# Decode attention on one core: 4 MB slabs of four kv heads in four slots, a softmax per two slabs, and the diagonal of PV picked on the vector engine

## The chip, the cores and the metric

The kernel runs on one core of a Trainium2 chip. The metric is the device time of one execution in microseconds. Most executions of a kernel agree within 0.3%; medians are quoted, and the state of each run (fast, slow, or unknown for a single run) is respected where kernels are compared. Ratios are the mean time of one kernel's fast runs over that of the other's fast runs in the same rounds on the same chip, so they are not quite the ratios of the medians quoted beside them.

## The reference

Two independent problems (A and B) of the same shape. Each is one decode step of attention with a sliding window:

```
B, Sq, D = 2, 1, 576;  Hq, Hkv, Sk, Dh = 32, 16, 16384, 128;  W = 4096
q = (x @ wq) as [B, Hq, 1, Dh]
k = repeat(k_cache[:, :, Sk-W:, :], 2)        # v likewise
scores = q k^T * Dh**-0.5;  p = softmax(scores);  o = p v
result = o as [B, 1, Hq*Dh] @ wo              # A and B joined on the last axis
```

Everything is bf16. The windows of K and V are 134 MB, the four weight matrices 19 MB. Each byte is used once, so the kernel is a stream of loads with some arithmetic beside it.

## The kernel before

All work is recorded as operations on five queues (PE tensor, DVE vector, ACT scalar, POOL, SP for the loads). The order of the `S.add` calls of one engine is the order in which that engine runs them; waits are derived from the dependency lists. A slab is one kv head of both batches: 128 rows of 16 KB, 2 MB. Slabs of K and V go through a ring of eight slots. A K slab is transposed in two halves on the vector engine (X), multiplied with the queries on PE (S); after four slabs comes one softmax (maximum, exponential, transpose of the probabilities pT); a V slab is multiplied seven slabs later (PV).

```python
    NR = 8; NXT = 3; LAG = 7           # ring slots, buffers for transposed halves, slabs between S and PV
        def make_X(t, jb):             # transpose of half a K slab: vector engine
            n = 2 * t + jb
            deps = [stream_dma[("K", t)]]
            if n >= NXT:
                pn = n - NXT
                deps.append(Sop[(pn // 2, pn % 2)])       # buffer free: three halves back
            ...
            Xop[(t, jb)] = S.add("dve", lambda e: e.transpose(xt[:, n % NXT, :].bitcast(FP32), ring[...]), deps, ...)
            if jb == 1:
                last_reader[("K", t)] = Xop[(t, jb)]      # the slot may be loaded again
        def make_S(t, jb): ...         # 8 matmuls of 512 columns, needs Xop[(t, jb)]
        def make_evac(G, pr):          # PV sums out of PSUM: scalar engine
            evac_op[(G, pr)] = S.add("act", lambda e: e.activation(oE[:, pr, :], OTB[:, :], ACTF.Copy, scale=rsb[...]), deps, ...)
        def make_dg(G):                # diagonal picked by 8 fp32 matmuls
            ...
        for t in range(NSLAB + LAG + 1):                  # NSLAB = 32
            i = t - LAG
            make_X(t, 0); make_S(t, 0)
            if Gc is not None: make_chain(Gc)             # every fourth step
            if Gp is not None: make_dg(Gp)                # every fourth step
            make_X(t, 1); make_S(t, 1)
            ...                                           # make_chain2, make_PV(i), make_chain3, make_evac, make_proj
```

(Conditions on `t` are left out in the loop.)

## Time and profile before

| | before |
|---|---|
| time, median | 367.23 us (367.14 to 367.76, three runs; 367.31 us over the four runs taken beside the kernel after) |
| span of the profiled run | 365.9 us |
| loaded | 153.1 MB |
| mid-kernel rate, 60 to 330 us | 427 GB/s, DMA share 1.01 |
| DVE busy | 51% |

These lines are from the page of the profiled run. In the slices each digit is the busy share of one fortieth of the span, in tenths; the line of queue q1 gives packets, MB and the share of the 16 DMA engines' span; a group's line gives busy us, mean ns of one, and then the engine's idle time just before these instructions and what ended it.

```profile
span 365.9 us, 3683 instructions
...
PE 273.0 (75%) x1700; PEld 101.6 (28%) x1435; DVE 185.8 (51%) x189; ACT 34.3 (9%) x114; POOL 14.2 (4%) x53
...
DMA  8999999999999999999999999999999999999995
...
q1 hardware_dynamic: 11236, 153.10, 98.7%
...
DMA 81%; DVE 12%; PE 5%; ACT 1%; issue 1%; SPq 0%
...
L436 DVE STREAM_TRANSPOSE xt<-ring 128x2048 f32<-128x2048 f32 x64 | 144.3, 2286 | 84.5 <-DMA ring<-in_A_k_cache_dram 43.3
```

The DMA engines work from the second slice to the last but one. The vector engine's transposes (L436) sit idle 84.5 us, and what ends it is a landing of K: the engine waits for data, and data come as fast as they can. The windows view (busy us per engine, PE clock, DMA share, GB/s) of mid-kernel says it in one line:

```profile
60.00:330.00 270.00, 211.75 (x1072) 75.27 (x856) 149.51 (x143) 23.41 (x79) 7.04 (x24) 0.82 1.01 427
```

### The profile page before, as it was taken

Reading aid. Unit: us, or ns where it says so; the run is one execution under the profiler, and the core shown is the slowest. Engines: PE = TensorE matmul, PEld = TensorE weight load, DVE = VectorE, ACT = ScalarE, POOL = GpSimd, SP = SyncE. Lnnn points to the kernel's source line nnn. Section 1 sums busy time; section 2 is a strip of 40 time slices with the busy share of each in tenths; the row PEclk is TensorE's granted clock in tenths of the full one; section 3 lists DMA queues with packets and bytes.
Section 4 is the critical chain, followed back from the end, with each engine's and each line's share of the span. In section 5 each row is a group of like instructions: output and inputs, shape, how many; then the busy total and the mean of one; then the engine's idle time right before and its main releaser. Section 6 shows DMA issues by size and latency. Waiting matters only on the chain.

```text
span 365.9 us, 3683 instructions
## 1 busy us (share of the span) xinstructions
PE 273.0 (75%) x1700; PEld 101.6 (28%) x1435; DVE 185.8 (51%) x189; ACT 34.3 (9%) x114; POOL 14.2 (4%) x53
## 2 busy tenths in 40 slices
PE   0635874967859888597867688596797977597796
PEld 0311111112215322252213232152224322143544
DVE  2105988955743675436644477405764467234100
ACT  1011002002000020002000020000300020002100
POOL 5010000000000000000000000000000000000000
PEclk9998999896995889858998869859897689959959
DMA  8999999999999999999999999999999999999995
GB/s 323 451 410 428 430 428 422 436 424 424 430 424 430 428 430 428 421 430 429 428 424 433 428 426 424 428 426 428 430 424 425 428 430 430 424 427 426 427 414 205
DMA packets 11264, 153.34 MB, mean 419 GB/s; under 512 B 1256, under 2 KB 1392, under 8 KB 2032
## 3 DMA queue, kind: packets, MB, share of 16 engines
q1 hardware_dynamic: 11236, 153.10, 98.7%
q8 instruction: 12, 0.20, 0.2%
q14 instruction: 4, 0.03, 0.0%
q10 hardware_dynamic: 12, 0.01, 0.0%
HBM read 153.10 MB, written 0.00 MB: 418 GB/s over the span
## 4 chain that ended last, share of the span: by engine, by line
DMA 81%; DVE 12%; PE 5%; ACT 1%; issue 1%; SPq 0%
DMA ring<-in_B_k_cache_dram 41%; DMA ring<-in_A_k_cache_dram 28%; DVE xt L436 11%; DMA wob<-in_B_wo_dram 8%; DMA ring<-in_A_wq_dram 4%; PE st L460 1%; PE st L380 1%; PE ot L273 1%; PE tb L619 1%; ACT pR L511 1%; PE pj L682 0%; DVE pT L530 0%; SPq L372 0%; PE tb L500 0%; DVE out_sb L692 0%
## 5 line engine op out<-in xcount | busy, mean ns | idle before, releaser
L436 DVE STREAM_TRANSPOSE xt<-ring 128x2048 f32<-128x2048 f32 x64 | 144.3, 2286 | 84.5 <-DMA ring<-in_A_k_cache_dram 43.3
L460 PE MATMUL st<-xt,zq 128*128 128x512 bf16 x256 | 114.7, 448 | 60.1 <-DVE xt L436 60.0
L380 PE MATMUL st<-xt,zq 128*128 128x512 bf16 x256 | 114.9, 449 | 0.0
L460 PEld LDWEIGHTS st<-xt,zq 128*128 128x128 bf16 x256 | 28.4, 111 | 154.7 <-DVE xt L436 82.8
L584 PE MATMUL ot<-ring,pT 128*32 128x512 bf16 x448 | 57.2, 407 | 0.7 <-ACT oE L609 0.7
L584 PEld LDWEIGHTS ot<-ring,pT 128*32 128x32 bf16 x448 | 21.0, 102 | 35.5 <-issue 18.4
L619 PEld LDWEIGHTS tb<-selv,oE 128*128 128x128 f32 x112 | 22.1, 293 | 6.0 <-issue 4.2
L619 PE MATMUL tb<-selv,oE 128*128 128x16 f32 x112 | 21.0, 335 | 0.8 <-ACT oE L609 0.8
L423 POOL TENSOR_TENSOR zq<-qs,bmask 128x64 bf16<-128x64 bf16 x32 | 9.3, 294 | 272.3 <-PE st L380 173.9
L638 DVE TENSOR_TENSOR oA<-tb,cmask 128x256 bf16<-128x256 f32 x7 | 3.0, 425 | 30.7 <-PE tb L619 30.7
L609 ACT ACTIVATE oE<-ot,rsb 128x512 f32<-128x512 f32 x14 | 9.6, 685 | 76.9 <-PE ot L584 76.9
L511 ACT ACTIVATE pR<-st,bias_sb 128x256 bf16<-128x256 f32 x32 | 15.9, 544 | 0.3
L470 DVE TENSOR_REDUCE mx<-st 128x2 f32<-128x512 f32 x16 | 10.0, 664 | 2.6 <-PE tb L650 2.6
L682 PE MATMUL pj<-wob,oP 128*2 128x288 bf16 x126 | 10.1, 305 | 0.9 <-DMA wob<-in_B_wo_dram 0.6
L530 DVE STREAM_TRANSPOSE pT<-pR 128x512 bf16<-128x512 bf16 x16 | 10.4, 686 | 0.0
L654 ACT ACTIVATE oP<-tb 128x16 bf16<-128x16 f32 x8 | 1.5, 191 | 92.7 <-PE tb L650 92.7
L254 PE MATMUL tb<-ident_b,xt 2*128 2x2 bf16 x36 | 2.3, 194 | 9.9 <-DVE xt L221 9.9
L504 ACT ACTIVATE bias_sb<-tb 128x2 f32<-128x2 f32 x8 | 1.4, 172 | 89.2 <-PE tb L500 89.2
L500 PE MATMUL tb<-ones_f,nMrep 1*128 1x1 f32 x32 | 5.2, 263 | 6.1 <-DVE nMrep L494 6.1
L593 PEld LDWEIGHTS st<-pT,ring 128*128 128x128 bf16 x256 | 7.2, 100 | 6.2 <-DMA ring<-in_B_v_cache_dram 6.1
L593 PE MATMUL st<-pT,ring 128*128 128x16 bf16 x256 | 7.6, 172 | 1.4 <-DMA ring<-in_B_v_cache_dram 1.3
L485 DVE TENSOR_REDUCE nM<-tb 1x8 f32<-1x64 f32 x16 | 2.7, 207 | 11.4 <-PE tb L476 11.4
(67 smaller groups left out, 89.6 us busy)
## 6 DMA issues: line engine op xcount, KB each, us to landing
ring<-in_A_k_cache_dram SPq DMA_DIRECT2D x16, 2048.0 KB, 33.1
ring<-in_A_v_cache_dram SPq DMA_DIRECT2D x16, 2048.0 KB, 35.1
ring<-in_B_k_cache_dram SPq DMA_DIRECT2D x16, 2048.0 KB, 35.8
ring<-in_B_v_cache_dram SPq DMA_DIRECT2D x15, 2048.0 KB, 35.2
ring<-in_A_wq_dram SPq DMA_DIRECT2D x1, 4608.0 KB, 13.4
ring<-in_B_wq_dram SPq DMA_DIRECT2D x1, 4608.0 KB, 23.8
wob<-in_A_wo_dram SPq DMA_DIRECT2D x4, 1152.0 KB, 32.4
wob<-in_B_wo_dram SPq DMA_DIRECT2D x3, 1152.0 KB, 30.4
```

The source lines that it names most:

```text
L380: return e.add_instruction(mybir.InstMatmult(name=nc.get_next_instruction_name(), engine=mybir.EngineType.PE, ins=[e.lower_ap(mv), e.lower ...
L423: return e.tensor_tensor(dst, src, msk, ALU.mult)
L436: Xop[(t, jb)] = S.add("dve", lambda e: e.transpose(xt[:, n % NXT, :].bitcast(FP32), ring[:, r, jb * HW_:(jb + 1) * HW_].bitcast(FP32)), d ...
L460: last = e.matmul(st[bk][:, 0:512], wt, mv, start=first, stop=True, skip_group_check=True)
L470: mxs = [S.add("dve", lambda e, jb=jb: e.tensor_reduce(mx[:, jb, :], st[jb][:, :].rearrange("p (x t) -> p t x", t=2), AX.X, ALU.max), [Sop ...
L511: last = e.activation(pR[:, jb, :].rearrange("p (x t) -> p t x", t=2)[:, t, :], st[jb][:, :].rearrange("p (x t) -> p t x", t=2)[:, t, :], ...
L530: chain[(G, "pT%d" % jb)] = S.add("dve", lambda e, jb=jb: e.transpose(pT[:, v, 512 * jb:512 * jb + 512].rearrange("p (w j q) -> p j w q", ...
L584: last = e.matmul(OTB[32 * c:32 * c + 32, :], pT[:, v, col:col + 32], ring[:, r, j * 128:(j + 4) * 128], start=(j % 32 == 0), stop=(j % 32 ...
L593: last = e.matmul(OL[m % 2][:, 0:16], ring[:, r, j * 128:(j + 1) * 128], pT[:, v, col:col + 16], start=(j == 0), stop=(j == KR - 1))
L609: evac_op[(G, pr)] = S.add("act", lambda e: e.activation(oE[:, pr, :], OTB[:, :], ACTF.Copy, scale=rsb[:, v, pr:pr + 1]), deps, "oE%d_%d" ...
L619: last = e.matmul(bank[:, 0:16], oE[:, pr, 128 * c:128 * c + 128], selv[:, pr, c, :], start=(pr == 0 and c == 0), stop=(pr == 1 and c == 3))
L682: last = e.matmul(PJ[half], oP[:, v, j, :], wob[:, v, j, half * NH:(half + 1) * NH], start=(proj_start(G) and j == 0), stop=True, skip_gro ...
```

## The change

The intent: fewer and larger loads (32 slabs of 4 MB with 32 KB rows), fewer small instructions. A slab is now four kv heads of one batch. There are four slots of 4 MB instead of eight of 2 MB, two buffers for transposed halves (of twice the size) instead of three, and one softmax per two slabs. The PV sums are no longer copied by the scalar engine and put through 112 fp32 matmuls: the vector engine multiplies them by a mask of the diagonal while it empties PSUM, and adds up. The core of the diff (start-up, masks, weights and the emission of waits are cut):

```diff
-    NR = 8
-    NXT = 3
-    LAG = 7
+    NSLOT = 4
+    LAG = 3
...
-            src = src_t[:, g, Sk - W:Sk, :].rearrange("b (r j) d -> r b (j d)", j=KR)        # 16 KB rows
+            src = src_t[b, 4 * g:4 * g + 4, Sk - W:Sk, :].rearrange("k (r j) d -> r k j d", j=KJ)  # 32 KB rows
...
+        def make_X(t, jh):
+            deps = [stream_dma[("K", t)][0][2], Sop[(t - 1, jh)] if t >= 1 else op_xT]
+            Xop[(t, jh)] = dve(lambda e: e.transpose(
+                xt[:, jh, :].bitcast(FP32).rearrange("p (kp x kt) -> p x kp kt", kp=2, kt=2),
+                ring[:, r, jh * HW_:(jh + 1) * HW_].bitcast(FP32).rearrange("p (x kp kt) -> p x kp kt", kp=2, kt=2)), ...)
...
+        def make_bias(G):
+            n, bk, op = tb_job(lambda e, bank: e.transpose(bank[:, 0:1], nMrep..., ident_f[0:1, 0:1]), ...)   # PE
+            b4 = dve(lambda e: e.scalar_tensor_tensor(bias4[:], vmask[:], bk[:, 0:1], offm[:], ALU.mult, ALU.add), [op, ...], ...)
...
+        def make_evac(i):
+            evac_op[i] = dve(lambda e: e.scalar_tensor_tensor(tv, o, rsb[:, v, b:b + 1], dm, ALU.mult, ALU.mult), deps, "ev%d" % i)
+            ch[(G, "red%d" % b)] = dve(lambda e: e.tensor_reduce(oR[:, b, :], tmp..., AX.X, ALU.add), ...)
...
+        def make_dg(G):
+            n, bank, op = tb_job(lambda e, bank: e.matmul(bank[:, 0:256], selx..., oR..., start=True, stop=True), ...)   # PE
+            a = dve(lambda e: e.tensor_tensor(tmp[:, 0:256]..., bank[:, 0:256]..., cm16..., ALU.mult), [op, d_cm, ch["tmp"]], ...)
+            ch[(G, "oP")] = dve(f_pick, [a] + ..., "oP%d" % G)
...
+        for t in range(NSLAB + LAG):          # NSLAB = 16
+            i = t - LAG
+            if live:
+                make_X(t, 0)
+                make_S(t, 0)
+            if Gb is not None:                # even steps
+                make_bias(Gb)
+            if Gd is not None:                # odd steps
+                make_dg(Gd)
+            if live:
+                make_X(t, 1)
+                make_S(t, 1)
+                ...
+            if live and odd:
+                make_max(t // 2)
+            if Gb is not None:
+                make_rsum(Gb)
+                make_pT(Gb)
+                make_sums(Gb)
+            ...
+            if i >= 0:
+                make_PV(i)
+                make_evac(i)
+            ...                               # make_proj
+            if live and odd:
+                make_Tm(t // 2)
```

## The prediction

> **What bounds the kernel now.** The DMA engines. The page's slices show them 90% or more busy in 37 of 40; the queue table gives the load queue 98.7% of the 16 engines' span; 153.1 MB are read. In the windows view, 60 to 330 us runs at 427 GB/s with a DMA share of 1.01: no hole in mid-kernel to win back. The compute engines are not close: PE 75% busy (its matmuls overlap), DVE 51%, ACT 9%. In the chain of waits DMA holds 81% of the span, and the DVE transposes on it release a ring slot while some 35 us of loads are already queued (issue to landing, median 33 to 36 us). Edges: first load issued at 0.8 us; last landing 363.45 us; then 2.5 us of projection, copy and store.
>
> So 950 fewer tensor instructions buy nothing by themselves. The bytes stay; 64 slabs of 2 MB become 32 of 4 MB. What can change is the price of a row, the feeding of the queue, and the tail.
>
> **Row price.** In the trace's DMA records a 16,384-byte row takes 613 ns on its engine (median), a 36,864-byte row (wq) 1364, a 9,216-byte row (wo) 351. A line through the first two is 12 ns + bytes/27.3 GB/s, and gives 350 for the third. A 32,768-byte row should take about 1214 ns (estimate from that line) against 2 x 613. Each engine moves about 512 of the 16 KB rows: 256 pairs x 12 ns = 3.1 us, plus 32 fewer completion writes of 9 ns = 0.3 us. Sum -3.4 us, all on the critical path. The Trainium skill, "DMA: Bandwidth & Descriptors", section "Where 436 GB/s comes from", puts the ceiling at 435.2 GB/s, 1.9% above the 427 here, so little more is to be had.
>
> **Feeding.** Four slots of 4 MB hold as many bytes as eight of 2 MB. A K slab is free after two transposes of 4096 fp32 (4.6 us each, from 2286 ns for 2048), a V slab after its PV, about 4 us. A 4 MB slab takes 9.8 us to load, and three slabs sit between a slab and its successor in the slot, so at release some 15 to 20 us of loads are queued. At the start the margin is smaller (estimated 7 us), still positive. I expect no starving.
>
> **Compute.** S keeps 512 matmuls of 512 columns, PV becomes 512; the fp32 selection (112 matmuls, 21 us) and the last group's 256 go. DVE gains, per two slabs, two evacuations and two reductions of 512 (about 0.68 us each) and a pT transpose of 2048 (about 2.3 us): from 186 to about 205 us, 56%. Off the path.
>
> **Tail.** Now wo 6 follows the last V and its projection stands before the last diagonal step on PE; the last projection starts about when the last part lands and runs all 16 matmuls then: +0.5 us (estimate).
>
> **Sum.** 367.2 - 3.4 + 0.5 = 364.3 us. Range 362.3 to 367.2. Faster by over 2%: 0.03; within 2%: 0.93; slower by over 2%: 0.04.
>
> **What would show it.** Right: 32 KB records near 1214 ns; mid-kernel 430 to 432 GB/s at share 1.0; DVE about 55%, PE 65 to 70% busy; the chain mostly DMA; last landing near 360 us and some 3 us of tail. Wrong: a mid-kernel DMA share under 0.98 (starving; the queue's own waits would name transposes or PV), or 32 KB records much above 1214 ns.
>
> **What would make it wrong.** One engine's rows now jump by 4 MiB between heads instead of 64 MiB between batches; HBM may like that more or less. The transposes walk an interleaved pattern (pairs of fp32); at half speed DVE would become the bound. Half as many slots may stall the queue in the first 100 us.

## The result, and the profile after

The time rose to 438.73 us (437.7 to 440.07); the ratio to before is 1.1944 (1.191 to 1.1979).

The same lines of the page, for the kernel after:

```profile
span 437.3 us, 2617 instructions
...
PE 247.6 (57%) x1299; PEld 60.3 (14%) x937; DVE 214.6 (49%) x138; ACT 44.4 (10%) x77; POOL 21.6 (5%) x82
...
DMA  8999999999995898949989498967989497895900
...
q1 hardware_dynamic: 6628, 153.10, 83.3%
...
PE 52%; DVE 36%; DMA 8%; POOL 1%; ACT 1%; issue 1%; SPq 0%; DVEq 0%
...
L448 PE MATMUL st<-xt,zq 128*128 128x512 bf16 x256 | 132.3, 517 | 151.7 <-DVE xt L422 151.7
L422 DVE STREAM_TRANSPOSE xt<-ring 128x4096 f32<-128x4096 f32 x32 | 141.5, 4431 | 20.4 <-DMA ring<-in_A_k_cache_dram 18.5
...
L542 DVE TENSOR_REDUCE oR<-tmp 128x128 f32<-128x512 f32 x16 | 16.4, 1026 | 0.6
```

No engine is near full: DMA 83%, PE 57%, DVE 49%. The DMA is full for about the first third and then has holes. The chain of waits has changed hands, from DMA 81% to PE 52% and DVE 36%. The score matmuls (L448) stand idle 151.7 us in front of a transpose. The transposes themselves (L422) wait for a load once, at the start. So data lie ready, and nobody is slow; the engines wait for one another. Mid-kernel in the windows view:

```profile
60.00:330.00 270.00, 154.26 (x768) 36.49 (x560) 141.42 (x85) 30.23 (x49) 12.25 (x46) 0.79 0.88 369
```

Which of the vector engine's instructions wait, and for whom (the view of waits, vector engine only; us in total, times, longest us):

```profile
DVE mx L456 <- PE st L242: 44.3, 8, 6.5
DVE tmp L551 <- PE tb L548: 43.6, 8, 7.1
DVE bias L474 <- PE tb L471: 39.7, 8, 6.0
DVE ssum L504 <- PE tb L501: 24.5, 7, 3.8
DVE tmp L541 <- PE ot L520: 19.5, 16, 2.5
DVE xt L422 <- DMA ring<-in_A_k_cache_dram: 18.5, 1, 18.5
```

All but the last line is waiting for PE; the last is the first load. The timeline of the vector engine over two steps shows why that matters (start us, us, engine, line, operation; in brackets the idle time in front and what ended it). Four names recur in it. The bias is the negated maximum of a softmax, brought back to all partitions through PE. The evacuation (L541, L542) empties the PV sums out of PSUM and adds up. The mask and pick (L551, L558) choose the diagonal, after one more matmul. A score block is the group of score matmuls (16 in this kernel) that follows one transpose.

```profile
204.32 4.42 DVE L422 STREAM_TRANSPOSE xt<-ring 128x4096 f32<-128x4096 f32 x1
214.21 0.23 DVE L474 SCALAR_TENSOR_TENSOR bias<-vmask,tb,offm 128x4 f32<-128x4 f32 x1 [5.47 <-PE tb L471]
214.36 4.44 DVE L422 STREAM_TRANSPOSE xt<-ring 128x4096 f32<-128x4096 f32 x1
219.49 2.31 DVE L490 STREAM_TRANSPOSE pT<-pR 128x2048 bf16<-128x2048 bf16 x1 [0.69 <-ACT pR L481]
225.43 0.17 DVE L504 TENSOR_REDUCE ssum<-tb 128x2 f32<-128x8 f32 x1 [3.63 <-PE tb L501]
...
227.28 0.75 DVE L541 SCALAR_TENSOR_TENSOR tmp<-ot,rsb,dmask 128x512 f32<-128x512 f32 x1 [1.49 <-PE ot L520]
228.07 1.02 DVE L542 TENSOR_REDUCE oR<-tmp 128x128 f32<-128x512 f32 x1
229.01 4.43 DVE L422 STREAM_TRANSPOSE xt<-ring 128x4096 f32<-128x4096 f32 x1
240.36 0.42 DVE L551 TENSOR_TENSOR tmp<-tb,cm 128x256 f32<-128x256 f32 x1 [6.92 <-PE tb L548]
240.82 0.61 DVE L558 TENSOR_REDUCE oP<-tmp 128x16 bf16<-128x256 f32 x1
241.35 4.43 DVE L422 STREAM_TRANSPOSE xt<-ring 128x4096 f32<-128x4096 f32 x1
251.33 1.23 DVE L456 TENSOR_REDUCE mx<-st 128x2 f32<-128x1024 f32 x1 [5.55 <-PE st L242]
253.19 0.75 DVE L541 SCALAR_TENSOR_TENSOR tmp<-ot,rsb,dmask 128x512 f32<-128x512 f32 x1 [0.63 <-PE ot L520]
...
255.53 4.42 DVE L422 STREAM_TRANSPOSE xt<-ring 128x4096 f32<-128x4096 f32 x1
```

The second transpose of the slab (214.36) has had its data since before the first one began, and its buffer was free. It starts 0.15 us after the bias, because on this engine it stands behind the bias. The bias waits for PE, PE has put the bias behind the first score block, and the first score block starts when the first transpose ends (208.74). In odd steps the mask of the diagonal (240.36) holds the same place. At the end of a step the evacuation waits for PV, PV stands behind the second score block, and the next transpose stands behind the evacuation. So transposes and score blocks take turns: in the two steps from 204.32 to 255.53 (51.2 us) the vector engine works 26.5 us and waits 24.7 us for PE and ACT (sum of the brackets). The loads of two steps take 41.9 us: that is the time of the same bytes (eight 2 MB slabs and one wo part) in the kernel before, whose chain repeats every 37.4 + 4.5 us. The profiled span grew by 71.4 us. The loop is not at this pace from the start: between the first transposes at 100.75 and 357.94 us, five pairs of steps took 51.4 us each on average, 48 us more than five times 41.9. By the DMA records the last byte of wo came 53.5 us later than before, counted from the first byte of wq (415.0 against 361.5 us), and the output's store ended 20.04 us after that byte instead of 2.17. The two make up the 71.4 us: the loads were held back, and then compute that had fallen behind them was still to be done.

The Trainium skill, "Perfetto Trace Analysis", section "Tensor Engine Instruction (MATMUL, LD_WEIGHTS)", says of the execution queues: "ACT/DVE/GPSIMD are strict FIFO". The trace agrees: the ready transpose waits 5.6 us (208.74 to 214.36) behind the bias here, and the bias waits 5.0 us on average over the eight even steps (39.7 us in all).

### The profile page after: what moved, and what is told of

It is laid out like the page before. It is cut to its first block, busy times and chain, and to the rows that moved or that the text cites. A ratio compares the mean times of both kernels' runs of the same rounds, so it can differ in the third digit from the quotient of the medians.

```text
span 437.3 us, 2617 instructions
## 1 busy us (share of the span) xinstructions
PE 247.6 (57%) x1299; PEld 60.3 (14%) x937; DVE 214.6 (49%) x138; ACT 44.4 (10%) x77; POOL 21.6 (5%) x82
## 4 chain that ended last, share of the span: by engine, by line
PE 52%; DVE 36%; DMA 8%; POOL 1%; ACT 1%; issue 1%; SPq 0%; DVEq 0%
DVE xt L422 30%; PE st L448 20%; PE st L242 18%; DMA ring<-in_A_k_cache_dram 8%; PE ot L520 8%; DVE oR L542 2%; PE pj L583 2%; PE pj L242 2%; DVE tmp L541 1%; ACT pR L481 1%; PE tb L548 1%; DVE oP L558 1%; POOL zq L414 1%; PE tb L501 1%; DVE tmp L551 1%
## 5 line engine op out<-in xcount | busy, mean ns | idle before, releaser
L448 PE MATMUL st<-xt,zq 128*128 128x512 bf16 x256 | 132.3, 517 | 151.7 <-DVE xt L422 151.7
L422 DVE STREAM_TRANSPOSE xt<-ring 128x4096 f32<-128x4096 f32 x32 | 141.5, 4431 | 20.4 <-DMA ring<-in_A_k_cache_dram 18.5
L242 PE MATMUL st<-xt,zq 128*128 128x512 bf16 x256 | 129.1, 504 | 0.0
L481 ACT ACTIVATE pR<-st,bias 128x512 bf16<-128x512 f32 x32 | 39.7, 1402 | 305.6 <-DVE bias L474 305.6
L448 PEld LDWEIGHTS st<-xt,zq 128*128 128x128 bf16 x256 | 31.0, 121 | 280.1 <-DVE xt L422 160.7
L520 PE MATMUL ot<-ring,pT 128*32 128x512 bf16 x512 | 33.9, 412 | 0.0
L456 DVE TENSOR_REDUCE mx<-st 128x2 f32<-128x1024 f32 x8 | 9.8, 1225 | 44.3 <-PE st L242 44.3
L551 DVE TENSOR_TENSOR tmp<-tb,cm 128x256 f32<-128x256 f32 x8 | 3.4, 425 | 43.6 <-PE tb L548 43.6
L490 DVE STREAM_TRANSPOSE pT<-pR 128x2048 bf16<-128x2048 bf16 x8 | 18.5, 2311 | 9.8 <-ACT pR L481 9.8
L541 DVE SCALAR_TENSOR_TENSOR tmp<-ot,rsb,dmask 128x512 f32<-128x512 f32 x16 | 12.0, 751 | 19.5 <-PE ot L520 19.5
L474 DVE SCALAR_TENSOR_TENSOR bias<-vmask,tb,offm 128x4 f32<-128x4 f32 x8 | 1.8, 227 | 39.7 <-PE tb L471 39.7
L542 DVE TENSOR_REDUCE oR<-tmp 128x128 f32<-128x512 f32 x16 | 16.4, 1026 | 0.6
L583 PE MATMUL pj<-wob,oP 128*2 128x288 bf16 x63 | 15.8, 286 | 0.5 <-DVE oP L558 0.5
L242 PE MATMUL pj<-wob,oP 128*2 128x288 bf16 x63 | 15.8, 286 | 0.0
L275 PE MATMUL ot<-ring,pT 128*32 128x512 bf16 x36 | 8.3, 448 | 3.3 <-DMA ring<-in_B_wq_dram 2.8
L481 ACT ACTIVATION_READ_ACCUMULATOR pR<-st,bias 128x1 f32 x32 | 8.7, 271 | 0.0
```

The costliest lines, as they stand in the source:

```text
L242: return e.add_instruction(mybir.InstMatmult(name=nc.get_next_instruction_name(), engine=mybir.EngineType.PE, ins=[e.lower_ap(mv_), e.lowe ...
L275: last = e.matmul(o, wt, mv_, start=first, stop=True, skip_group_check=True)
L422: Xop[(t, jh)] = dve(lambda e: e.transpose(xt[:, jh, :].bitcast(FP32).rearrange("p (kp x kt) -> p x kp kt", kp=2, kt=2), ring[:, r, jh * H ...
L448: last = e.matmul(ob, wt, mv_, start=first, stop=True, skip_group_check=True)
L456: ch[(G, "max")] = dve(lambda e: e.tensor_reduce(mx[:], st[:, :].rearrange("p (x t) -> p t x", t=2), AX.X, ALU.max), [Sop[(2 * G + 1, 1)]] ...
L481: last = e.activation(pR[:].rearrange("p (x k) -> p k x", k=4)[:, kv, :], st[:, :].rearrange("p (x t) -> p t x", t=2)[:, kv % 2, :], ACTF.Exp,
```

## The experiments

The theory (**serial loop**): the order of instructions on the vector engine makes transposes and score blocks alternate, and the loop of compute is then longer than the loads. The rivals: **A**, four slots of 4 MB let the load queue run dry; **B**, the work moved to the vector engine is too much for it; **C**, the tensor engine's clock falls in the gaps and that is the whole loss. Where a run has "rounds", it was timed in fast runs against the kernel before; a single look has an unknown state, which is good enough for the differences of 5% and more that are read from it; experiment 8 reads a smaller one (1.2%), and is weaker for it.

### 1. The second transpose first

```diff
                 make_X(t, 0)
                 make_S(t, 0)
+                make_X(t, 1)
             if Gb is not None:
                 make_bias(Gb)
             if Gd is not None:
                 make_dg(Gd)
             if live:
-                make_X(t, 1)
                 make_S(t, 1)
```

PE's order is the same; the vector engine's differs by this one place.

> Only the order of the vector engine changes: both transposes of a K slab stand ahead of the small vector operations that wait for the tensor engine (bias in even steps, pick of the diagonal in odd steps). Theory, serial loop: transpose and score matmuls alternate in the kernel after (two steps of 51.2 us, where the loads need 41.9 us). With the second transpose over the first score block, two steps need some 38 us of compute, less than the loads, so DMA is full again: 364 to 368 us, mid-kernel DMA share 1.0. Rival A, slots: four slots of 4 MB let the queue run dry whatever the order: still above 410 us. Rival B, the work added to the vector engine (picks, reductions, longer exp): nothing is removed here, so still above 410 us.

Measured: 369.1 us (367.42 to 370.02), ratio 1.002 (0.9993 to 1.0048). One moved line takes back all of the loss within the noise (the interval of the ratio holds 1). Mid-kernel:

```profile
60.00:330.00 270.00, 178.83 (x926) 43.97 (x675) 175.81 (x104) 35.47 (x57) 14.04 (x51) 0.78 1.00 430
```

The vector engine now does more in the same 270 us (175.8 us busy against 141.4 in the kernel after), because all its work fits. Rivals A and B fall: the slots and the work are those of the kernel after. The tensor clock is 0.78 here, no higher than in the kernel after (0.79), which already speaks against rival C: in this order the slow clock does not hold back the loads. The expected range was missed by 1 us; the reason is the tail (experiment 5): the store ends 8.9 us after the last byte of wo, against 2.2 us before.

### 2. Half of each V slab

```diff
-            cuts = [(0, KJ, ring_sem[r])]
+            cuts = [(0, KJ if kind == "K" else KJ // 2, ring_sem[r])]    # all V slabs but the last; PV still multiplies all of it
```

> The kernel after, with only half of each V slab loaded (except the last slab): wrong result on purpose, 31 MB of 153 MB less to load, all instructions of the engines unchanged. Serial loop: the loads do not set the pace after the first slabs, so the time stays within 3% of 438 us. Rival A, slots or late loads: the queue has a quarter less to do per step (41.9 us per two steps become about 32), so the time falls to 380 us or less.

Measured: 438.83 us (one run, result wrong). With a fifth of the bytes gone the time lies inside the spread of the kernel after (437.7 to 440.07). So loads do not set the pace there, and an account of it that starts from slow or late loads does not fit.

### 3. Even steps only, odd steps only

```diff
                 make_S(t, 0)
+                if not odd:                    # the other run: if odd:
+                    make_X(t, 1)
```

> The kernel after, with the second transpose moved ahead in even steps only (ahead of the bias operation). Serial loop: the first score block of even steps (5.1 us) hides behind the second transpose (4.4 us): 8 times about 5 us saved, near 395 us.

> The kernel after, with the second transpose moved ahead in odd steps only (ahead of the diagonal's mask and pick). Serial loop: odd steps save the first score block (5.8 us) or the transpose behind it and the diagonal step's 1.6 us, about 6 to 7 us each: near 385 us. Neither half alone should reach the loads' pace; if one of them does all the work of both, the loop is not what I think.

Measured: 406.08 us and 396.19 us (one run each): 33 and 43 us saved, each 11 us less than expected. The sum, 75 us, is about the whole loss of 71, but the estimates per step were too large, and that the two savings add was not shown. The trace of the even-step run shows one reason. The vector engine there:

```profile
188.98 8.75 DVE L422 STREAM_TRANSPOSE xt<-ring 128x4096 f32<-128x4096 f32 x2
198.75 0.23 DVE L474 SCALAR_TENSOR_TENSOR bias<-vmask,tb,offm 128x4 f32<-128x4 f32 x1 [1.02 <-PE tb L471]
204.06 2.31 DVE L490 STREAM_TRANSPOSE pT<-pR 128x2048 bf16<-128x2048 bf16 x1 [5.08 <-ACT pR L481]
```

The bias no longer waits 5.5 us, but the transpose of the probabilities now waits 5.1 us for the exponential, which starts at the bias and was hidden before. A wait taken out of a serial loop uncovers the next one. In the odd-step run two steps took 44.4 us, still more than 41.9.

### 4. The next slab's first transpose first

```diff
-                make_X(t, 0)
+                if t == 0:
+                    make_X(t, 0)
                 make_S(t, 0)
...
                 make_X(t, 1)
                 make_S(t, 1)
+                if t + 1 < NSLAB:
+                    make_X(t + 1, 0)
```

> Only the other reorder: the next slab's first transpose ahead of max, pT, sums and the evacuation; the second transpose still behind the bias or pick that waits for the first score block. Serial loop: now the second score block overlaps the next first transpose, and the evacuation leaves the loop; a step falls from 25.6 to about 17 to 20 us against 20.9 of loads, so again the loads bind: 362 to 369 us. If instead it stays above 390, the wait at bias and pick is the whole matter and not the alternation.

Measured: 369.37 us (367.7 to 371.57), ratio 1.0054 (1.0025 to 1.0083), 0.4 us above the expected range, with a tail of 7.8 us from the last byte of wo to the end of the store. Mid-kernel, and the wait of the bias:

```profile
60.00:330.00 270.00, 176.32 (x936) 42.65 (x680) 171.95 (x107) 35.27 (x57) 14.03 (x52) 0.84 1.00 430
...
DVE bias L474 <- PE tb L471: 31.5, 8, 5.6
```

Here the bias still stands in front of the second transpose and still waits for PE (31.5 us in all, 39.7 in the kernel after); it is enough that the other half of the alternation is broken. So the cause is the alternation, not one particular wait in it.

### 5. Both reorders, and then the tail

> Both reorders on the vector engine: the second transpose ahead of bias and pick, and the next slab's first transpose ahead of max, pT, sums and the evacuation. With the second transpose ahead alone the loads ended near 358.5 us (363.4 before), but the compute ran up to 10 us behind them, so the end came at 368.7. Serial loop with row price: now the transposes follow the landings, the last softmax is done before the last V slab lands, and the tail shrinks to 3 to 4 us: 361.5 to 364.5 us, 0.985 to 0.992 of before. Rival A, slots: if the four slots cost something of their own, the loads end later than 360 us and the time stays at 367 or above.

Measured: 366.26 us (366.13 to 368.72, six runs), ratio 0.9981 (0.9962 to 1.0001): 1.8 us above the expected range. The loads were as expected: the trace's DMA records put the last byte of wo 357.7 us after the first byte of wq, against 361.5 us before (359.5 and 363.4 us after the start of the span; the 358.5 us that the expectation gives for experiment 1 is 359.5 by the same records). The time after that byte was not: 5.1 us to the end of the output's store, against 2.2 before. The vector engine waits for loads again (compare the same view of the kernel after):

```profile
DVE xt L422 <- DMA ring<-in_B_k_cache_dram: 61.2, 8, 8.3
DVE xt L422 <- DMA ring<-in_A_k_cache_dram: 50.6, 6, 18.4
...
DVE bias L474 <- PE tb L471: 4.0, 5, 1.3
DVE mx L456 <- PE st L242: 3.1, 1, 3.1
```

The tail was late because on PE the PV of slab 13 stood behind the sums of the last softmax, and the last diagonal step behind the projection that waits for wo 6. Both are a matter of order once more (the edit also leaves out three filler matmuls, and its parts were not tested apart):

```diff
+            if t == NSLAB:
+                make_PV(i)
+                make_evac(i)
             if Gb is not None:
                 make_rsum(Gb)
                 make_pT(Gb)
                 make_sums(Gb)
...
-            if i >= 0:
+            if i >= 0 and t != NSLAB:
                 make_PV(i)
                 make_evac(i)
...
         filler(3)
-        make_proj(NG - 2)
         make_dg(NG - 1)
-        filler(3)
+        make_proj(NG - 2)
         make_proj(NG - 1)
```

> Both reorders of the vector engine, and the end put in another order: PV 13 and its evacuation ahead of the last group's sums and pT (it stood 10 us behind its landed slab, waiting for the last exponential), and the last diagonal step ahead of the projection that waits for wo 6. The loads end near 358.6 us in the version without this; its end came 6.4 us later. Row price and an intact tail: 2 to 4 us after the loads, 362.5 to 365 us, 0.985 to 0.993 of before. If the tail does not shrink, 366 us again.

Measured: 364.49 us (364.28 to 366.19, six runs), ratio 0.9933 (0.9914 to 0.9952); the store ends 3.2 us after the last byte of wo. This version is faster than both kernels, than the one before by 0.7%; it is the only one whose interval lies clear of 1 on the fast side. Lines of its page:

```profile
span 363.3 us, 2627 instructions
...
q1 hardware_dynamic: 6628, 153.10, 98.4%
...
DMA 68%; DVE 25%; PE 4%; ACT 1%; SPq 0%; issue 0%; POOL 0%
```

### 6. 16 KB rows with the same order

```diff
-            cuts = [(0, KJ, ring_sem[r])]
+            cuts = [(0, KJ // 2, ring_sem[r]), (KJ // 2, KJ, ring_sem[r])]   # X and PV wait for both
```

This is on top of both reorders, without the mended tail.

> Both reorders, with each 4 MB slab loaded by two transfers of 16 KB rows instead of one of 32 KB rows; same slots, same order of work. Row price: 256 more rows per engine at 12 ns and 30 more completion writes of 9 ns: 3.3 us longer than with 32 KB rows, 365 to 368 us. If rows of 32 KB bring nothing, the two are the same within 1 us.

Measured: 368.64 us (368.41 to 370.87, six runs) against 366.26 us with 32 KB rows in the same rounds: 2.4 us, where 3.3 were expected. (The time lies 0.6 us above the range of 365 to 368, which was built on the range that experiment 5 had missed.) From first to last loaded byte it is 360.1 against 357.7 us. In the DMA records the median row of 16 KB took 614 ns and that of 32 KB 1216 ns. The gain of the larger rows is real and small, and it was below the forecast by a quarter.

### 7. The tensor clock kept up

```diff
+        def warm(n):                   # n matmuls of 224 columns, constants in, unused columns of the projection's bank out
+            ...
                 make_X(t, 1)
+                warm(36)
                 make_S(t, 1)
...
+            if t + 1 < NSLAB:
+                warm(36)
```

> The kernel after in its own order, with 36 idle matmuls of 224 columns after each score block and at the end of each step, to keep the tensor clock up while the vector engine transposes. Serial loop with a slow clock in it: the four score blocks of two steps take about 3.5 us each instead of 5.0 to 5.8, so two steps fall by 5 to 7 us: 380 to 400 us. Rival C, the throttled tensor clock is the whole loss: 364 to 370 us. If the clock plays no part: 435 to 445 us.

Measured: 413.17 us (one run), with a mean clock of 0.97 mid-kernel instead of 0.79:

```profile
60.00:330.00 270.00, 221.92 (x1697) 36.74 (x604) 153.99 (x91) 30.40 (x49) 12.93 (x48) 0.97 0.92 388
```

Two steps took 44.6 to 47.8 us (first transposes at 154.55, 199.14, 243.72, 291.54 and 339.20) instead of 51.2. So the clock is a part of the loss, 26 us of 71 net of what the idle matmuls cost, and an effect of the alternation: PE stands idle while the vector engine transposes. In the trace of the kernel after, neighbouring matmuls of the first half of a score block start about 427 ns apart and later ones about 236 ns. The Trainium skill, "TensorE: Matmul & The Clock Gate", section "Part 1: The HAM clock gate", says that the clock halves after an idle window of about 3.4 us; in this trace PE idles 4.7 us in front of the block at 208.80, the granted clock on record is 0.5 from 208.29 to 211.71 us and then 1.0, and the factor is 1.8. The time is above the range of 380 to 400: only some pairs of steps fell by the 5 to 7 us expected, others by 3.5, and the first 150 us took as long as without the idle matmuls (154.55 against 152.98 us at the same transpose). The trace shows why the start gained nothing: in the first steps the loads had run ahead, and the idle matmuls stood in front of score blocks that were ready (a stretch of them from 52.04 us on, the block behind it at 55.39, its transpose done at 50.60); the first maximum came at 66.58 us instead of 58.56. Rival C falls: with the clock up the kernel is still 12% slower than before.

The result was wrong, which was not intended. The idle matmuls wrote only unused columns, but with the start flag.

```diff
-                last = e.matmul(o, ones_b[:, :], mv, start=True, ...)
+                last = e.matmul(o, ones_b[:, :], mv, start=first, ...)        # first: only before any PV; same for the held ones
```

> The same idle matmuls as in the run whose result was wrong, but without the start flag on all but the first of them. If the wrong result came from the start flag clearing the accumulation state of the whole bank in which the projection sums up, the result is now right, and the time is the same as there, 410 to 416 us.

Measured: correct, 411.16 us (one run). The Trainium skill, "PSUM — Partial Sum Buffer", section "The four PSUM rules", says that a first matmul clears the accumulation state of the whole 2 KiB bank on the quadrants it writes, not of its columns alone. These two runs agree: relative error 0.479 with the flag, correct without it.

### 8. The reduction of the pick left out

```diff
-            ch[(G, "red%d" % b)] = dve(lambda e: e.tensor_reduce(oR[:, b, :], tmp..., AX.X, ALU.add), ...)
+            ch[(G, "red%d" % b)] = evac_op[i]          # oR filled with a constant once
```

> The kernel after in its own order, without the 16 reductions of 512 that finish the pick of the diagonal on the vector engine (1.03 us each, 16.4 us busy); the result is wrong on purpose. Serial loop: each stands between an evacuation and the next transpose, so all of it comes off: 438.7 less 14 to 17 us, 421 to 425. If the vector engine's share of 49% meant slack, nothing comes off: 436 to 440.

Measured: 433.43 us (one run, wrong): 5.3 us saved of 16.4 us of work, where 14 to 17 us were expected. The traces show that none of it was saved in the loop. The last transpose of K, in the kernel after and here:

```profile
392.81 4.43 DVE L422 STREAM_TRANSPOSE xt<-ring 128x4096 f32<-128x4096 f32 x1
```

```profile
392.70 4.43 DVE L423 STREAM_TRANSPOSE xt<-ring 128x4096 f32<-128x4096 f32 x1
```

Up to there the two runs keep step, with 51.0 to 51.4 us per pair of steps in both from 153 to 357 us; the saving comes after, in the tail (15.1 us from the last byte of wo to the end of the store, 20.0 in the kernel after). One reason: in odd steps the next transpose stands behind the negated maximum (L464), which waits on PE behind the projection; without the reduction it only waits longer:

```profile
204.11 0.28 DVE L464 TENSOR_REDUCE nM<-tb 1x16 f32<-1x128 f32 x1 [0.31 <-PE tb L462]
```

```profile
203.57 0.28 DVE L465 TENSOR_REDUCE nM<-tb 1x16 f32<-1x128 f32 x1 [1.38 <-PE tb L463]
```

The wait in front grew from 0.31 to 1.38 us. In even steps the next transpose did come 0.9 us sooner after the one before it, and the wait of the mask fell from 6.92 to 6.12 us; but that of the maximum grew from 5.55 to 6.63 us and that of the bias from 5.47 to 6.07. The granted clock may be what takes the time back. On record it changes only at multiples of 3.41 us in both traces, the pair of 51.2 us is fifteen of these, and mid-kernel the clock is 0.77 here against 0.79. That the loop keeps step with these intervals was not tested. So the loop is not a plain sum of the durations in it, as the expectation took it to be. What stands is that the reductions are not what the kernel lost.

### 9. The alternation put into the kernel before

```diff
-            if n >= NXT:
-                pn = n - NXT
+            if n >= 1:
+                pn = n - 1
                 deps.append(Sop[(pn // 2, pn % 2)])
...
+            if jb == 0 and t - 1 - LAG >= 0:
+                deps.append(PVop[t - 1 - LAG])
```

> The kernel before (16 KB rows, eight slots, nothing of the change) with two waits added: each transpose waits for the score block just before it, and a slab's first transpose for the PV of the step before. That is the alternation of the kernel after, without its rows, slots or vector work. Serial loop: a 2 MB step of two transposes (2.3 us), two score blocks (2.6 us or more at the lower clock) and a PV (1.9 us) is 12 us or more against 10.5 us of loads: 400 to 460 us. If the loss of the kernel after came from slots, rows or the moved pick, this stays at 367 to 375.

Measured: 446.33 us, correct (one run). Its chain of waits is close to that of the kernel after (PE 52%, DVE 36%, DMA 8%), although its rows, slots, softmax and diagonal are those of before:

```profile
q1 hardware_dynamic: 11236, 153.10, 85.5%
...
PE 55%; DVE 35%; DMA 6%; issue 2%; ACT 1%; SPq 0%; DVEq 0%
```

So the alternation alone, in 2 MB slabs, costs this kernel 79 us. (The edit takes away the run-ahead of the third buffer and adds the wait for PV; the two were not tested apart.)

## Why the prediction was wrong

- **The step that failed is "Feeding": "I expect no starving".** It computed when a slot is released from durations alone (two transposes 9.2 us, PV 4 us), as if each transpose ran as soon as its data and buffer were there. It did not read where the transposes stand on their engine. The order was in the diff: in every step the bias or the mask, which wait for PE behind the first score block, stand between the two transposes, and the evacuation, which waits for PV behind the second, stands in front of the next. Two steps were 51.2 us of turns against 41.9 us of loads, the mid-kernel DMA share was 0.88, and the last byte of wo came 53.5 us later than before. Experiments 1 and 4 show that breaking the turns at either place brings the loads back to 430 GB/s; experiment 2 shows that loads did not set the pace; experiment 9 makes the loss in the other kernel.
- **"Compute ... Off the path" failed with it.** The busy shares were roughly right (DVE forecast about 205 us, measured 214.6; PE forecast 65 to 70%, measured 57% of a longer span), and they said nothing: an engine 49% busy was on the chain because of whom it waited for. In the kernel before, operations of this kind stood between two transposes once per four slabs, a third buffer let the transposes run ahead, and the evacuation was on the scalar engine. The change removed all three, as its diff shows (they were not tested one by one), and I counted only instructions.
- **My list of what could go wrong had the engine and not the mechanism.** It named slow transposes (they took 4435 ns for 4096 elements, against 4.6 us forecast from 2286 ns for 2048) and the slots. The sign that I offered for starving did appear, a DMA share under 0.98 with the queue's own waits at transposes and PV:

```profile
SPq L369 <- DVE xt L422: 254.0, 16, 20.3
SPq L369 <- PE ot L520: 53.2, 7, 8.1
```

I would have read it as a matter of slots, which experiment 1, with the same four slots, rules out.
- **"Row price" was right.** The median row was forecast at 1214 ns and measured at 1213 ns (kernel after) and 1216 ns (both reorders). Where loads bind, the load phase shrank by 3.7 us (361.5 to 357.8 us from first to last byte, best version) against 3.4 forecast; isolated in experiment 6 it was worth 2.4 us. Mid-kernel the rate was 430 GB/s. The ceiling of 435.2 GB/s that the prediction took from the skill was not exceeded by the mean rate of 60 to 330 us in any of these runs (at most 430).
- **"Tail +0.5 us" was too small.** It was +1.0 us with the order mended and +2.9 us with the order of the change, even once the loop was mended; in the kernel after itself it was +17.9 us (20.04 against 2.17), as compute ran behind the loads. The reduction that it counted at 0.68 us takes 1.03 us, but most of the 2.9 us is order again: PV 13 behind a softmax that it does not need, and the last diagonal step behind a projection.
- The sum, 364.3 us, was the time of the kernel with the orders mended (364.49 us), not of the kernel that was given. That it agrees so closely is partly luck: the loads gained 0.3 us more than forecast, and the tail lost 0.5 us more.

## What to carry to other kernels

Before trusting busy shares, write down each engine's instructions of one loop iteration in program order and walk the waits across engines: an instruction that waits holds back everything behind it on its engine, ready or not, and if A waits for B and then B for A in one iteration, they take turns instead of overlapping. When work is moved to an engine that prefetches or transposes for others, put the work that waits behind the work that feeds, and give it buffers enough to run ahead (more buffers were not tried here). When a profile shows no engine busy and the loads not full, look at the ready instruction that did not start and ask what stands in front of it.

## What the Trainium skill lacked or had wrong

- "DMA: Bandwidth & Descriptors" has times per transfer for loads issued from GpSimd, but no time per row, by its length, for loads issued from SP. Here a row took about 12 ns + bytes / 27.3 GB/s on its engine: 351 ns for 9,216 bytes, 613 for 16,384, 1213 for 32,768, 1364 for 36,864.
- "VectorE: DVE Perf Modes" gives reductions one element per cycle. The reduction with 128 outputs of 4 strided elements each took 1026 ns for 512 elements, where one with 2 outputs, reading PSUM, took 664 ns for 512; I found no page with times that separate these, and no run isolates the stride.
- "ScalarE: Activation LUTs" has no time for strided patterns that I found. The exponential took 1402 ns for 512 elements (writing every fourth bf16) and 544 ns for 256 (every second one), 2.6 times for twice the elements; no run isolates the stride.
- "VectorE: DVE Perf Modes" has no time for long fp32 transposes; elsewhere the skill has a rate for the engine's transpose, but I found no measured time. They took 2286 ns for 2048 in order, and 4435 ns for 4096 walked in pairs of fp32 in an interleaved pattern, which is under twice as long, so no cost of the pattern shows.
